# A new order table for attention and the first expert, and fewer preset instructions, in a one-core attention and expert kernel

## The chip, the cores and the metric

The kernel runs on one core of a Trainium2 chip. The metric is the device time of one execution in microseconds, as the median of several runs. Engines are named as in the profile: PE is the matmul engine, DVE the vector engine, ACT the scalar engine, POOL GpSimd, SP the engine that issues the DMAs.

## What is computed

Three stages follow each other: an attention with a coarse and a local part over 2 x 8 heads of 576 positions, a mixture of 8 experts over the 1152 tokens with a gate that is balanced over rows and columns, and one feed-forward layer. Cut to what matters:

```python
# attention, for each of 2 x 8 heads, q, k, v: 576 x 64
q_d, k_d, v_d = (t.reshape(B, H, S // 4, 4, D).mean(axis=3) for t in (q, k, v))
out_up = np.repeat(sm_attn(q_d, k_d, v_d), 4, axis=2)
mask = np.abs(pos[:, None] - pos[None, :]) < 4
out_local = softmax(np.where(mask, scale * q @ k.T, -1e9)) @ v
x = (out_up + out_local).transpose(0, 2, 1, 3).reshape(1152, 512)

# experts: D = 512, F = 1024, E = 8
P = np.exp(x @ w_gate - max)
for _ in range(8):
    P /= P.sum(1, keepdims=True) + 1e-9
    P /= P.sum(0, keepdims=True) + 1e-9
    P *= N / E
out = sum(P[:, e:e + 1] * (np.maximum(x @ w1[e], 0) @ w2[e]) for e in range(E))

# last layer: w_in 512 x 2048, w_out 2048 x 512
h = out @ w_in
return (h * np.tanh(np.log1p(np.exp(h)))) @ w_out
```

## The kernel before

Matrices are multiplied in half precision as a high and a low part each, scaled by powers of two that are found from the data: three products of parts stand for one product. Splitting a matrix takes an ACT instruction for the high part and a DVE instruction for the low part.

The change touches the first stage: attention, and the part of expert 0 that is woven into it. Its work is cut into some 500 **steps**, methods of the class Attention and a few functions beside it. A table, ORDER (line 911), lists them by name, and `run` (line 1346) emits them one after the other. Each engine has a queue of its own and works it off in order, so the table fixes the order on every engine and on the DMA queue of SP; what waits for what is left to semaphores. A name carries its numbers (`TP2.0.1`) and, behind a colon, the engine where there is a choice (`A` for ACT, `V` for DVE, `G` for POOL). The heads go in pairs j = 0 to 7, of which 0 to 3 are batch 0 and 4 to 7 batch 1.

- **LK, LQ, LW, LV**: loads of K and Q of a pair, of the windows of V, of V for the coarse part. **LD0.n, LD1.n, LD2.n**: halves of w1 of expert 0, w2 of expert 0, w1 of expert 1. **LG**: the gate. Tiles come from small pools (four for Q and K, four for V windows, two for raw weights), and a load waits until the tile that it takes over is done with.
- **TPj.n.i**: PE transposes half i of Q (n = 0) or K (n = 1). **TQ, TK** copy it out of PSUM, **SQ, SK** sum four neighbours for the coarse part.
- **QLj.0, .1, .2**: the local scores, 48 small matmuls for each of two heads. **LM, SU, EL, LS, LN, TR, BD**: softmax of these, its transpose and the blocks for the product with V. **QD, DM, ED, DS, DN, AP, AE**: the same for the coarse part.
- **AV, AD**: products with V. **VP, VE, VS, VG, VR, VQ**: coarse V, and what its scale is found from. **UP, XF, XH, XL**: sum of both parts, high and low part of x for this pair.
- **WG, WD, WM, WT, WP, WR, WQ, WE**: the scale of a matrix (squares by PE or ACT, greatest value by DVE, spread over the partitions by PE, powers of two by DVE). **WH, WL**: high and low part of a quarter of expert 0's weights.
- **Mf.c, Rf.c, Hf, If**: one product of the first layer of expert 0 (12 matmuls), its relu, high and low part of the result. They need x of the whole batch. **Nt.f, Et**: the second layer and its way out.
- **FLi**: fill steps. With `A` they do nothing, with `V` they are one matmul on the tile warm, with `G` two (line 1260).

Ahead of the table stand presets: constants on POOL (lines 1271 to 1290, among them an addition on the tile lib, L1290, in front of which POOL stands still) and the identity matrix, the mask and the pooling weights on DVE (emit_consts, from line 536). Behind the table come the rest of expert 0, the other experts and the last layer, which the change leaves alone.

Of the kernel before, what the change touches and what calls it, by code (L numbers as in the profile page):

```python
# [10 lines left out]
F32 = mybir.dt.float32  # L11
# [4 lines left out]
ALU = mybir.AluOpType  # L16
# [5 lines left out]
def attn_moe_moe2_kernel(ctx: ExitStack, tc: tile.TileContext, q, k, v, w_gate, w1, w2, w_in, w_out, out):  # L22
# [495 lines left out]
    pool_w = const.tile([128, 32], F32, name="pool_w")  # L518
    half = const.tile([128, 2], F32, name="half")
# [19 lines left out]
    def emit_consts(t, mask):  # L539
# [3 lines left out]
        nc.vector.memset(ident, 0.0)  # L543
# [6 lines left out]
        for i in range(4):  # L550
            p = slice(32 * i, 32 * i + 32)
            nc.vector.tensor_scalar(out=ident[p, p], in0=d[p, :], scalar1=0.0, scalar2=None, op0=ALU.is_equal)
# [7 lines left out]

# [3 lines left out]
        near = t[:, 5, 0:8]  # L564
        nc.vector.scalar_tensor_tensor(out=near, in0=col[:, 0:8], scalar=-4.0, in1=row[:, 0:8], op0=ALU.mult,
# [3 lines left out]
        for i in range(4):  # L569
            p = slice(32 * i, 32 * i + 32)  # L570
            nc.vector.tensor_scalar(out=pool_w[p, 6 * i:6 * i + 6], in0=near[p, 0:6], scalar1=4.0, scalar2=None,
                                    op0=ALU.is_lt)
# [24 lines left out]
    class Attention:  # L597
# [341 lines left out]


    mm_pools = []
    mm_n = [0]

    def mm_banks(n):
        i = len(mm_pools)
        mm_pools.extend([(ps_pool(f"mm{i}", n), f"mm{i}")] * n)

    def mm_tile():
# [811 lines left out]
```

## Time and profile before

| | us |
|---|---|
| median of 3 runs | 984.0 (983.19 to 984.54) |
| profiled execution | 987.67 |
| its span | 985.9 |
| PE busy in the span | 962.0 |
| DVE busy | 665.2 |
| ACT busy | 517.6 |

The profiled execution is one run beside the timed ones, and its span leaves out what lies ahead of the first instruction and behind the last. PE's busy time is the sum of its matmuls as the trace has them; what is left of the span is waiting. The order table ends at 117 us of the span.

### The profile page before, as it was taken

The numbers are of one execution on the slowest core, as the hardware profiler recorded it, in microseconds if no ns is written. First come the engines' busy times: TensorE is split into PE (matmuls) and PEld (weight loads), VectorE is DVE, ScalarE is ACT, GpSimd is POOL, SyncE is SP. The second block draws the span as 40 slices with busy tenths as digits, with TensorE's granted clock in tenths as the row PEclk, the third lists the DMA queues.
The fourth block names the chain that finished last, engine by engine and source line by source line (L and its number), as shares of the span: only waits on it lengthen the run. The fifth ranks groups of instructions, "written<-read, shape, count | busy, mean of one in ns | idle before, by whom it ended". The sixth has DMA issues, their size and how long they took to land. (4 is left out here: it accounts for less than half of the span.)

```text
span 985.9 us, 19187 instructions
## 1 busy us (share of the span) xinstructions
PE 962.0 (98%) x7925; PEld 653.4 (66%) x7928; DVE 665.2 (67%) x1333; ACT 517.6 (53%) x1000; POOL 60.2 (6%) x114
## 2 busy tenths in 40 slices
PE   6999999999999999999999999999999999999998
PEld 5766674774476467547645754674476667888897
DVE  5877578588677938775994888388756455545531
ACT  4757353766287447728654773567284232433431
POOL 5524200000000000000000000000000000000000
PEclk9999999999999999999999999999999999999999
DMA  8862202022423233240424423232204602000010
GB/s 209 167 146 100 94 6 86 1 87 67 147 88 105 64 137 122 65 155 27 140 65 150 128 66 132 69 120 65 107 4 162 263 1 86 12 12 22 7 60 33
DMA packets 82403, 88.15 MB, mean 89 GB/s; under 512 B 34572, under 2 KB 66700, under 8 KB 81036
## 3 DMA queue, kind: packets, MB, share of 16 engines
q1 hardware_dynamic: 82316, 86.93, 27.6%
q8 instruction: 62, 1.02, 0.4%
q14 instruction: 25, 0.20, 0.1%
HBM read 71.97 MB, written 14.94 MB: 88 GB/s over the span
## 5 line engine op out<-in xcount | busy, mean ns | idle before, releaser
L1124 PE MATMUL mm<-wbh,h 128*128 128x512 f16 x1152 | 353.7, 380 | 2.4 <-ACT h L587 2.4
L1124 PEld LDWEIGHTS <-h 128*128 128x128 f16 x1728 | 168.8, 98 | 196.1 <-ACT h L587 2.9
L1124 PE MATMUL mm<-wbl,h 128*128 128x512 f16 x576 | 219.1, 380 | 0.0
L1093 PE MATMUL mm<-x,wah 128*128 128x288 f16 x672 | 128.1, 286 | 0.0
L1059 DVE SCALAR_TENSOR_TENSOR r<-mm,s 128x288 f32<-128x288 f32 x168 | 75.0, 454 | 71.2 <-PE mm L1093 64.3
L1093 PEld LDWEIGHTS <-wx 128*128 128x128 f16 x1008 | 98.6, 98 | 30.6 <-issue 5.9
L1542 PE MATMUL mm<-xc,win 128*128 128x256 f16 (+1 forms) x960 | 107.6, 262 | 0.0
L1055 ACT ACTIVATE s<-mm 128x288 f32<-128x288 f32 x168 | 66.4, 413 | 75.9 <-PE mm L1093 75.6
L1093 PEld LDWEIGHTS <-wah 128*128 128x128 f16 x896 | 87.7, 98 | 26.5 <-issue 0.6
L1093 PE MATMUL mm<-xt,wx 128*128 128x288 f16 x672 | 97.0, 286 | 4.1 <-DVE r L1059 4.0
L1093 PE MATMUL mm<-x,wal 128*128 128x288 f16 x336 | 96.1, 286 | 0.0
L1542 PEld LDWEIGHTS <-win 128*128 128x128 f16 x960 | 87.2, 98 | 13.3
L1551 ACT ACTIVATE tt<-mm,cf 128x512 f32<-128x512 f32 (+1 forms) x40 | 25.8, 645 | 113.1 <-PE mm L1542 111.3
L1068 DVE SCALAR_TENSOR_TENSOR h<-r,h 128x576 f16<-128x576 f32 x112 | 81.5, 750 | 0.6 <-ACT h L1067 0.6
L1067 ACT ACTIVATE h<-r 128x576 f16<-128x576 f32 x112 | 74.3, 680 | 11.2 <-DVE r L1059 11.0
L1558 DVE TENSOR_TENSOR tt<-tt 128x128 f32<-128x128 f32 x128 | 31.6, 288 | 69.4 <-ACT tt L1551 68.3
L1157 DVE SCALAR_TENSOR_TENSOR acc<-mm,pc,acc 128x512 f32<-128x512 f32 x63 | 47.0, 746 | 33.4 <-PE mm L1124 33.2
L254 ACT ACTIVATE junk<-raw 128x1024 bf16<-128x1024 f32 x52 | 54.9, 1056 | 0.3
L98 POOL PARTITION_ALL_REDUCE ma<-m x25 | 11.4, 458 | 669.5 <-DVE m L258 385.8
L1093 PEld LDWEIGHTS <-wal 128*128 128x128 f16 x448 | 43.8, 98 | 11.1
L1093 PE MATMUL mm<-x,wx 128*128 128x288 f16 x336 | 50.3, 286 | 0.0
L428 ACT ACTIVATE junk<-w 128x512 bf16<-128x512 f32 x32 | 20.1, 629 | 57.2 <-DVE w L421 41.4
(265 smaller groups left out, 1383.8 us busy)
## 6 DMA issues: line engine op xcount, KB each, us to landing
raw<-in_moe_w_dram SPq DMA_DIRECT2D x32, 1024.0 KB, 6.0
f<-in_moe_w_in_dram SPq DMA_DIRECT2D x16, 512.0 KB, 3.7
f<-in_moe_w_out_dram SPq DMA_DIRECT2D x16, 512.0 KB, 3.4
scr<-st SPq DMA_DIRECT2D x32, 256.0 KB, 2.3
scri<-st SPq DMA_DIRECT2D x16, 256.0 KB, 2.5
win<-scri SPq DMA_DIRECT2D x2, 2048.0 KB, 7.6
vw<-in_v_dram SPq DMA_DIRECT2D x30, 96.0 KB, 5.1
qk<-in_k_dram SPq DMA_DIRECT2D x16, 144.0 KB, 3.7
```

Source lines behind the costliest of these rows:

```text
L254: nc.scalar.activation(out=junk, in_=r[:, c * 1024:(c + 1) * 1024], func=AF.Square, accum_out=mx[:, 2 * i + c:2 * i + c + 1])
L428: nc.scalar.activation(out=b, in_=w, func=AF.Square, accum_out=mq[:, f // 8:f // 8 + 1])
L1055: nc.scalar.activation(out=t, in_=ps, func=AF.Copy, scale=HSC)
L1059: nc.vector.scalar_tensor_tensor(out=out, in0=ps, scalar=HSC, in1=r, op0=ALU.mult, op1=ALU.add)
L1067: lows.append((n + 3, lambda: nc.scalar.activation(out=hi, in_=r, func=AF.Relu)))
L1068: lows.append((n + 6, lambda: nc.vector.scalar_tensor_tensor(out=lo, in0=r, scalar=0.0, in1=hi, op0=ALU.max, op1=ALU.subtract)))
L1093: nc.tensor.matmul(ps, lhsT=w.part(wi, a)[:, c:c + 128], rhs=factor(b, bn, xi, i), start=(not before and k == 0), stop=(k == 5), skip_grou ...
L1124: nc.tensor.matmul(ps, lhsT=h[ft][:, hi, t * 128:(t + 1) * 128], rhs=wt[:, ws], start=(ft == 0 and n == 0), stop=(ft == FT - 1 and n == 2))
L1157: nc.vector.scalar_tensor_tensor(out=a, in0=ps, scalar=pc[:, t:t + 1], in1=a, op0=ALU.mult, op1=ALU.add)
L1542: nc.tensor.matmul(ps[:, q_ * n:(q_ + 1) * n], lhsT=win[q_][:, wi, f, ws], rhs=x[:, xi, kk, :], start=(m == 0), stop=(m == 3 * KT - 1))
L1551: nc.scalar.activation(out=tt[:, 0:2 * n], in_=ps, func=AF.Mish, scale=coef[c][:, f:f + 1])
L1558: nc.vector.tensor_tensor(out=a[o], in0=a[u], in1=a[v], op=op)
```

## The change

ORDER gets a new text with the same 511 steps: all 30 fill steps are in it, but four of them now issue five matmuls together, where six issued seven. Steps move in the table, and some change their engine: five more TQ, four TK and two SQ are on DVE, one SK, one AE and one H fewer. The presets are rewritten: the identity matrix and the pooling weights are made in one instruction each from a pattern of 32 columns and a tile block that says which rows belong to which 32; the tile warm is set on DVE instead of POOL, half comes from block, and the POOL instructions stand in another order with lib ahead of most. The table, cut to its first line on both sides:

```diff
+    block = const.tile([128, 4], F32, name="block")
...
-        nc.vector.memset(ident, 0.0)
...
-        for i in range(4):
-            p = slice(32 * i, 32 * i + 32)
-            nc.vector.tensor_scalar(out=ident[p, p], in0=d[p, :], scalar1=0.0, scalar2=None, op0=ALU.is_equal)
+        near = t[:, 5, 0:32]
+        nc.vector.tensor_scalar(out=near, in0=d, scalar1=0.0, scalar2=None, op0=ALU.is_equal)
+        nc.vector.tensor_tensor(out=ident.rearrange("p (b c) -> p b c", b=4), in0=near.unsqueeze(1).to_broadcast([128, 4, 32]),
+                                in1=block.unsqueeze(2).to_broadcast([128, 4, 32]), op=ALU.mult)
...
+        nc.vector.memset(warm, 1.0)
...
-        for i in range(4):
-            p = slice(32 * i, 32 * i + 32)
-            nc.vector.tensor_scalar(out=pool_w[p, 6 * i:6 * i + 6], in0=near[p, 0:6], scalar1=4.0, scalar2=None,
-                                    op0=ALU.is_lt)
+        nc.vector.tensor_scalar(out=near, in0=near, scalar1=4.0, scalar2=None, op0=ALU.is_lt)
+        nc.vector.tensor_tensor(out=pool_w[:, 0:24].rearrange("p (b c) -> p b c", b=4),
+                                in0=near.unsqueeze(1).to_broadcast([128, 4, 6]),
+                                in1=block.unsqueeze(2).to_broadcast([128, 4, 6]), op=ALU.mult)
...
-        "LK0 TP0.1.0 LQ0 FL5:V LK1 TP0.1.1 TP0.0.1 LK2 TP0.0.0 TK0.1:A TK0.0:A FL23:G LQ1 LD0.1 TQ0.1:A LQ2 TQ0.0:V "
...
+        "LK0 TP0.1.1 TP0.1.0 LQ0 LQ1 TK0.1:A TP0.0.0 TQ0.0:V TP0.0.1 TK0.0:A LK1 TQ0.1:V LD0.1 QL0.0 QL0.1 QL0.2 "
...
-        nc.gpsimd.memset(warm, 1.0)
-        nc.gpsimd.memset(half, 0.0)
+        lib = pools["keep"].tile([128, 16], F32, name="lib")
+        nc.gpsimd.memset(block, 0.0)
         for i in range(4):
-            nc.gpsimd.memset(half[32 * i:32 * i + 32, i % 2:i % 2 + 1], 1.0)
-        nc.gpsimd.memset(ones, 1.0)
-        nc.gpsimd.memset(ss, 0.0)
-        nc.gpsimd.memset(pool_w, 0.0)
+            nc.gpsimd.memset(block[32 * i:32 * i + 32, i:i + 1], 1.0)
+        nc.gpsimd.memset(lib, 0.0)
+        nc.gpsimd.memset(pool_w[:, 24:32], 0.0)
...
+        nc.gpsimd.tensor_tensor(out=lib[:, 0:8], in0=lib[:, 0:8], in1=lib[:, 8:16], op=ALU.add)
+        nc.gpsimd.tensor_tensor(out=half, in0=block[:, 0:2], in1=block[:, 2:4], op=ALU.add)
+        for i in range(2):
+            nc.gpsimd.memset(keep["ad"][i].rearrange("p h a g c -> p (h a g) c")[:, :, 24:32], 0.0)
+        nc.gpsimd.memset(ones, 1.0)
+        nc.gpsimd.memset(ss, 0.0)
         emit_fields()
-        lib = pools["keep"].tile([128, 16], F32, name="lib")
-        nc.gpsimd.memset(lib, 0.0)
-        nc.gpsimd.tensor_tensor(out=lib[:, 0:8], in0=lib[:, 0:8], in1=lib[:, 8:16], op=ALU.add)
```

What this does to the engines' queues is shown at three places. First the DMA queue of SP from its start, before (qk are the tiles of Q and K, raw those of weights, vw the V windows):

```order
L607 DMA qk<-in_k_dram 96x6x64 x2
L607 DMA qk<-in_q_dram 96x6x64 x2
L607 DMA qk<-in_k_dram 96x6x64 x4
L607 DMA qk<-in_q_dram 96x6x64 x2
L158 DMA raw<-in_moe_w_dram 128x2x1024
L607 DMA qk<-in_q_dram 96x6x64 x2
L626 DMA vw<-in_v_dram 29x64
L626 DMA vw<-in_v_dram 32x11x64
L626 DMA vw<-in_v_dram 32x12x64 x3
L158 DMA raw<-in_moe_w_dram 128x2x1024
L607 DMA qk<-in_k_dram 96x6x64 x2
```

And the same queue in the new order:

```order
L608 DMA qk<-in_k_dram 96x6x64 x2
L608 DMA qk<-in_q_dram 96x6x64 x4
L608 DMA qk<-in_k_dram 96x6x64 x2
L158 DMA raw<-in_moe_w_dram 128x2x1024 x2
L608 DMA qk<-in_k_dram 96x6x64 x2
L608 DMA qk<-in_q_dram 96x6x64 x2
L608 DMA qk<-in_k_dram 96x6x64 x2
L627 DMA vw<-in_v_dram 29x64
L627 DMA vw<-in_v_dram 32x11x64
L627 DMA vw<-in_v_dram 32x12x64 x11
L608 DMA qk<-in_q_dram 96x6x64 x4
```

Both halves of w1 now stand ahead of K2 and Q2, and three V windows ahead of Q4 and Q3. Second, PE from its start, before (at and aty are the PSUM tiles of transposes, fill that of the fill steps, att that of the scores):

```order
L704 MATMUL at<-ident,qk 128x96 x3
L1263 LDWEIGHTS warm
L1263 MATMUL fill<-warm 128x512
L704 MATMUL aty<-ident,qk 128x96 x6
L704 MATMUL at<-ident,qk 128x96 x3
L1263 LDWEIGHTS warm
L1263 MATMUL fill<-warm 128x512
```

And the same in the new order:

```order
L705 MATMUL aty<-ident,qk 128x96 x3
L705 MATMUL at<-ident,qk 128x96 x6
L705 MATMUL aty<-ident,qk 128x96 x3
L737 LDWEIGHTS ident_82
L737 MATMUL att<-mask,ident_82 128x192
```

The fill matmuls between the first transposes and the scores are gone. Third, DVE in front of the last low part of x of batch 0 (x<-xf, four instructions, the last is XL3; wal are low parts of w1, sl softmax steps), before:

```order
L243 SCALAR_TENSOR_TENSOR wal<-raw,sc_w_0_705,wah 128x1024
L764 TENSOR_TENSOR sl<-att,lmx 128x384
L889 TENSOR_TENSOR xf<-att,up 128x2x6x48
L899 SCALAR_TENSOR_TENSOR x<-xf,sx_1051,x 128x576 x3
L889 TENSOR_TENSOR xf<-att,up 128x2x6x48
L243 SCALAR_TENSOR_TENSOR wal<-raw,sc_w_0_705,wah 128x1024
L899 SCALAR_TENSOR_TENSOR x<-xf,sx_1051,x 128x576
```

And in the new order:

```order
L765 TENSOR_TENSOR sl<-att,lmx 128x384
L900 SCALAR_TENSOR_TENSOR x<-xf,sx_1074,x 128x576
L1171 TENSOR_REDUCE m_1180<-wg_r 128x1
L900 SCALAR_TENSOR_TENSOR x<-xf,sx_1074,x 128x576
L890 TENSOR_TENSOR xf<-att,up 128x2x6x48
L110 TENSOR_REDUCE mrow<-at 1x1
L890 TENSOR_TENSOR xf<-att,up 128x2x6x48
L900 SCALAR_TENSOR_TENSOR x<-xf,sx_1074,x 128x576 x2
```

Two low parts of w1 that stood here have moved further ahead, and a step for the gate's scale (mrow) stands between.

## Rows read from the trace of the kernel before

**Rows 1.** The page: the span's busy times and instructions of each engine.

```profile
PE 962.0 (98%) x7925; PEld 653.4 (66%) x7928; DVE 665.2 (67%) x1333; ACT 517.6 (53%) x1000; POOL 60.2 (6%) x114
```

**Rows 2.** Stages: stretch in us, length, busy us (instructions), PE clock, DMA share, GB/s.

```profile
0.00:20.00 20.00, 13.42 (x285) 10.40 (x286) 12.20 (x45) 8.37 (x24) 8.88 (x44) 0.91 0.86 216
20.00:40.00 20.00, 16.78 (x426) 13.63 (x424) 14.39 (x36) 13.31 (x43) 11.76 (x14) 0.91 0.80 164
40.00:52.00 12.00, 10.97 (x345) 8.52 (x344) 11.72 (x22) 9.45 (x23) 5.22 (x7) 1.00 0.98 221
52.00:62.00 10.00, 7.70 (x81) 5.58 (x81) 5.82 (x12) 5.58 (x19) 2.98 (x5) 0.83 1.17 227
62.00:117.00 55.00, 55.00 (x746) 35.66 (x742) 41.97 (x83) 31.53 (x80) 19.19 (x19) 1.00 0.17 57
```

**Rows 3.** PE's timeline: start, duration, line, tiles, count, wait in front with releaser.

```profile
23.40 0.69 PE L743 MATMUL att<-kt,qt 64*32 64x32 f32 x43 [2.18 <-issue]
...
33.27 0.25 PE L743 MATMUL att<-kt,qt 64*32 64x32 f32 x4 [0.51 <-issue]
...
52.55 0.41 PE L969 MATMUL mm<-x,wah 128*128 128x288 f16 x2
...
57.10 0.28 PE L969 MATMUL mm<-x,wal 128*128 128x288 f16 x1 [2.30 <-issue]
...
117.02 2.35 PE L1192 MATMUL lp<-wg_hl,x 128*128 128x16 f16 x80
```

**Rows 4.** Three more stretches, in the columns of rows 2.

```profile
23.39:57.09 33.70, 29.34 (x756) 23.40 (x759) 29.73 (x63) 23.60 (x66) 16.34 (x20) 0.95 0.90 195
...
50.00:57.09 7.09, 4.79 (x131) 3.65 (x128) 6.91 (x12) 4.59 (x16) 2.68 (x5) 1.00 1.19 281
...
57.50:60.90 3.40, 3.40 (x18) 2.40 (x16) 0.76 (x1) 2.22 (x5) 0.00 (x0) 0.52 1.20 200
```

**Rows 5.** The page: instruction queue (packets, MB), and loads by tile (issues, KB each).

```profile
q8 instruction: 62, 1.02, 0.4%
...
raw<-in_moe_w_dram SPq DMA_DIRECT2D x32, 1024.0 KB, 6.0
...
vw<-in_v_dram SPq DMA_DIRECT2D x30, 96.0 KB, 5.1
qk<-in_k_dram SPq DMA_DIRECT2D x16, 144.0 KB, 3.7
```

**Rows 6.** Start: the first K load's issue, the time that such loads take, PE, POOL.

```profile
0.72 0.94 SPq L607 DMA_DIRECT2D qk<-in_k_dram  x2
...
DMA to landing us min/median/max: 2.6/2.6/2.6
...
4.15 0.71 PE L704 MATMUL at<-ident,qk 96*128 96x96 f32 x3 [4.15 <-DVE mask_t L556]
...
10.80 0.20 POOL L1290 TENSOR_TENSOR lib<-lib 128x8 f32<-128x8 f32 x1 [7.47 <-DVE lmx L759]
```

**Rows 7.** PE's timeline at full clock: two TP, mask, QL part, AP.

```profile
39.13 0.83 PE L704 MATMUL at<-ident,qk 96*128 96x96 f32 x6
39.80 0.33 PE L736 MATMUL att<-mask,ident 128*128 128x192 bf16 x2
40.06 0.35 PE L743 MATMUL att<-kt,qt 64*32 64x32 f32 x32
40.34 0.46 PE L844 MATMUL at<-ident,ad 72*96 72x72 f32 x4
```

**Rows 8.** DVE from 30.4 to 52.5 us by line: count, busy us, mean ns.

```profile
L243 DVE SCALAR_TENSOR_TENSOR wal<-raw,sc_w,wah 128x1024 f16<-128x1024 f32 x4 | 5.4, 1344 | 0.0
L899 DVE SCALAR_TENSOR_TENSOR x<-xf,sx,x 128x576 f16<-128x576 f32 x4 | 3.1, 805 | 0.0
L889 DVE TENSOR_TENSOR xf<-att,up 128x576 f32<-128x576 f32 x4 | 3.0, 745 | 0.2 <-ACT up L587 0.2
```

**Rows 9.** PE's waits from 110 to 165 us: line, releaser, total us, count, longest.

```profile
PE mm L1124 <- ACT h L587: 2.4, 1, 2.4
```

More of the change, by code (lines that the diff above doesn't have):

```diff
@@ L559, in emit_consts @@
         nc.scalar.activation(out=mask, in_=edge.unsqueeze(1).to_broadcast([128, G, 32]), func=AF.Copy)
+        nc.vector.memset(warm, 1.0)
         nc.vector.memset(mask[0:32, 0, 0:3], SHUT)
         nc.vector.memset(mask[96:128, G - 1, 27:32], SHUT)
-        near = t[:, 5, 0:8]
-        nc.vector.scalar_tensor_tensor(out=near, in0=col[:, 0:8], scalar=-4.0, in1=row[:, 0:8], op0=ALU.mult,
+        near = t[:, 5, 0:6]
+        nc.vector.scalar_tensor_tensor(out=near, in0=col[:, 0:6], scalar=-4.0, in1=row[:, 0:6], op0=ALU.mult,
                                        op1=ALU.add)
@@ L1282, in attn_moe_moe2_kernel @@
             nc.gpsimd.memset(keep["qt"][i][:, S:S + 8], 0.0)
-            nc.gpsimd.memset(keep["ad"][i].rearrange("p h a g c -> p (h a g) c")[:, :, 24:32], 0.0)
         A = [Attention(b, pools, at_tile, at2_tile) for b in range(B)]
```

52 rows, old and new, of the table ORDER are left out of this document.

## The prediction

> **What bounds the kernel now.** I read the page first, then the stages, then what stops PE. TensorE is busy 962.0 of 985.9 us at almost full clock [rows 1], so some 24 us of idle time are there to win, and the change reaches only those ahead of the gate's matmuls at 117.0 us, where the order table ends [rows 3]. The stages [rows 2] tell where they lie. From 62 to 117 us PE is busy 55.00 of 55.00: no order wins there. From 0 to 40 us PE has 30.2 us of work and the DMA engines are 0.86 and 0.80 busy: this part goes at the pace of the loads. From 40 to 52 us DVE is busy 11.72 of 12: VectorE sets the pace, since the first product of expert 0 needs all of x of batch 0, whose last low part (XL3) is DVE work. From 52 to 62 us PE is busy 7.70 of 10 at a clock of 0.83, with DVE at 5.82: something else stops PE. [Rows 3] show it: 2.18 us of standstill in front of 23.40, 2.30 us in front of 57.10, each in the middle of a run of equal matmuls and waiting for no engine ("issue"). Between the two stand 1515 loads and matmuls [rows 4], six times 252; queue q8 brings 62 instruction packets of 16 KB [rows 5] for PE's 15,853 loads and matmuls [rows 1], 256 to a packet. Both stops are ends of an instruction block whose successor had not come.
>
> On this the Trainium skill (Runtime: NRT & Kernel Launch, section Instruction fetch mechanics) also has blocks of 16 KiB or 256 instructions, but calls their crossing mostly hidden. The trace agrees on the block, not on the hiding: [rows 3] have 2.30 us in the open. By that rule nothing of the kind would stand in the new order and term 3 below would be -4.0, which is a rival's value; by the rows it hangs on what the loads do just then.
>
> **The presets.** ident took five DVE instructions and takes two now. But the first transposes, at 4.15 us, also need the first K load, whose second half is issued at about 1.2 us and takes 2.6 us or a little more [rows 6]: it is there close to 4 us. I take 0, between 0 and -0.3. POOL comes free for attention only at 10.80, behind 7.5 us of standstill in front of lib [rows 6]; lib stands some 1 us earlier in the new order, but about 1 us of memsets (ad, ones, ss, the fields) has moved behind it: 0. The two fill matmuls fewer ran where PE was waiting anyway.
>
> **The loads up to 36 us.** The new table takes both halves of expert 0's w1 ahead of K2 and Q2. Sizes are in [rows 5]: a Q or K load is two of 144 KB, a V window four of 96 KB, a half of w1 1024 KB. Ahead of TP2.0.1 now stand six Q/K loads and two halves, 3.87 MB. At the 216 GB/s of the first 20 us, or the 190 of the first 40 [rows 2], that is 17.9 to 20.4 us: PE will stand idle in front of TP2.0.1, where it was working before. It then has 8.6 us of work up to TP3.0.1, which needs Q3: 5.93 MB, 29.8 to 31.2 us. From there 4.1 us to TP4.1.1, which needs K4: 6.91 MB, 35.8 to 36.4 us. (PE work is counted by steps, start to start in [rows 7]: 0.33 for a TP, 0.28 for a QL part, 0.26 for its mask; by the same timeline about 0.3 for AP, 0.64 for AD and QD, 0.85 AV, 0.6 VP, 0.4 VG, 1.0 WG.) At 36.1 us the kernel before has 20.8 us of table work done, the new one 19.1 to 19.5: it is behind here, not ahead.
>
> The wait in front of TP2.0.1 also drops the clock, as the 2.30 us did before: [rows 4] have 0.52 between 57.5 and 60.9. The same again is 1.7 us, and lies under the wait for Q3, so I take 0. The Trainium skill (TensorE: Matmul & The Clock Gate, Part 1) says that the array is throttled until activity releases it, which speaks against dropping fill matmuls; the clock rows agree with it, and by the rule alone the sum would be 1.7 us worse.
>
> **VectorE up to the first product.** From TQ3.1, behind Q3, the new table has these DVE steps up to and with XL3: three low parts of w1 at 1.34 us, four XL at 0.80, four XF at 0.75 [rows 8], four TQ, a pooled sum, two transposes, the softmax steps and the scale of x: 21.7 us by the trace's durations. The same count for the kernel before, from 30.4 us (LS2) to XL3's end at 52.45, gives 22.2, and it took 22.1. So the first product comes 21.6 us behind about 30.9, at 52.5 us, as before (52.55, [rows 3]). **Term 1: 0**, from -1.5 (Q3 at 29.8, DVE without a gap) to +1.5 (Q3 at 31.2, and waits of DVE on PE). By its own work PE is there at 51.3 and does not decide.
>
> **Behind the first product.** The PE work left is 0.3 us more: two transposes (TP6.0.0, TP6.0.1) have moved behind it, the pair WQ3 ahead of it. **Term 2: +0.3.**
>
> The stop at 57.10 cost 2.30 us and then the clock, 0.83 over ten us or 1.7 us [rows 2]: 4.0 together. Counting loads and matmuls, the same block begins in the third product (M0.1) now, in the second (also M0.1) before. The one ahead of it begins near 50 us in both: [rows 4] have 259 loads and matmuls from 50.00 to 57.09, in the new order TP6.1.1 stands there. So it took 7.1 us from the crossing to the next block, of which PE's work filled some 4.5. Now the need comes at 52.5 + 2.9 = 55.4 instead of 54.8. The loads just then are the same: half of w2 (LD1.0), LW5, LQ7. LW5 waits for AV3, near 47.7; LD1.0 can go a little ahead of it, so its data is perhaps half a us earlier. The block then comes at 56.5 to 57.0, and 1.1 to 1.6 us of the stop stay, and the clock with it. **Term 3: -1.2**, between -4.0 (the block is in time) and +0.3 (later by that). The stop at 23.40 goes, since the block behind QL1.2 arrives while PE waits for Q2; it lay under the loads and is worth 0.
>
> VectorE has more to do: five TQ, four TK, two SQ have moved to it, less has left, some 5 us net, most in expert 0's first stage. Up to TK7.0, which QL7.0 needs, DVE has 22.4 us by prices, PE 24.4. From 62 to 117 us it was busy 41.97 of 55 [rows 2]; now it needs nine tenths of the time up to there. **Term 4: +0.3** for PE waiting on it, from 0 to 2.5.
>
> From 117 us on the code is the same, and what stops PE there, 2.4 us for ACT h [rows 9], comes from an order that starts from the same place: 0.
>
> **Sum**: 0 + 0.3 - 1.2 + 0.3 = -0.6 us. The profiled execution took 987.67 us around a span of 985.9; the median of the three timed ones is 984.0. The terms are differences of parts, so they go on the median: 983.4.
>
> **Rivals.** *The block is in time.* If LD1.0 is through by 50 us, or PE crosses into the block ahead when it is, the next block comes while PE works through this one, as at the crossings between the two stops, the worst of which cost 0.51 us at 33.27 [rows 3], and term 3 is -4.0: 0.3 - 4.0 + 0.3 = -3.4, and with term 1 between -1.5 and +0.5 from -4.9 to -2.9, so 979.1 to 981.1. For it: in the new order DMA has a gap near 42 us (LW4 waits for AV0), so less stands in the queues. Against it: LQ6, LW6 and LV4 are ahead of LD1.0. *VectorE is late.* Slower than before: the copies moved from ACT to DVE stand in line behind low parts of 1.3 us; Q3 comes at 31.2 or later, XL3 ends at 54 (+1.5), and in the first stage PE waits for TK7.0 and for banks (+2); with the stop as it was, 1.5 + 0.3 - 0.5 + 2 = +3.3, between +2 and +4.5: 986 to 988.5. It decides once DVE's gaps between 18 and 52 us have grown by more than 1.5 us.
>
> **How the numbers follow.** The forecast, part of the stop remaining, covers -2.6 to +1.5 us and gets 0.50; the block in time 0.32; VectorE late 0.18. A measurement of this kernel tells some 0.2%, 2 us, from no change: faster is below 982.0, slower above 986.0. The forecast has 0.08 below 982.0 and 0.42 within; the block in time lies below; of VectorE late 0.01 is within. Faster 0.40, same 0.43, slower 0.17. The range goes from 978.6, half a us beyond the first rival's end for the presets and faster loads, to 986.6 in the slower case; some 0.2 stays outside. The forecast's own range is 981.4 to 985.5.
>
> **What would show it.** In the profile after: an idle PE in front of TP2.0.1, near 18 us, as its longest wait in the first 40 us; the first product (mm from x and wah) between 51 and 54 us; an "issue" wait of 1 to 2 us in the third product, then a clock of one half; DVE over 0.85 busy from there to 80 us; the gate's matmuls at 116 to 117 us. I am wrong on the loads if TP2.0.1 starts before 17 us or Q3 is there before 29; on VectorE if the first product comes by 50 or after 55; on the block if there is no "issue" wait over 0.5 us behind the first product, and then the time is the first rival's. If all these agree and the time does not, the difference lies behind 117 us, where I have put 0.

## The result: 0.5% slower, and the profile after

The changed kernel took 989.28 us (median of five, 988.51 to 991.05) against 984.0 before (five, 982.85 to 985.6): a ratio of 1.0055, 95% interval 1.0039 to 1.007. A second comparison, later and with twelve runs of it and 35 of the kernel before, gave 988.59 against 985.16 us, 1.0021 with 0.9998 to 1.0043. The range of the prediction ended at 986.6, and no change or a small gain had been the likely case. By the medians the change is a loss of 3 to 5 us. The ratios take in all runs and not the medians alone, and the second interval just reaches no change, so the sign of the loss is surer than its size.

The busy times of the page say nothing of it; in the columns of [rows 1]:

```profile
PE 963.2 (98%) x7923; PEld 654.7 (66%) x7926; DVE 665.8 (67%) x1340; ACT 513.6 (52%) x990; POOL 53.8 (5%) x112
```

The stages do; in the columns of [rows 2], and one more stretch, 15 to 25 us:

```profile
0.00:20.00 20.00, 11.91 (x247) 9.20 (x247) 10.39 (x36) 5.25 (x15) 6.43 (x41) 1.00 0.94 223
20.00:40.00 20.00, 17.01 (x329) 13.26 (x332) 13.58 (x38) 12.35 (x34) 8.25 (x12) 0.91 0.75 147
40.00:52.00 12.00, 10.81 (x319) 8.21 (x321) 10.51 (x25) 7.15 (x23) 9.42 (x11) 1.00 0.56 120
52.00:62.00 10.00, 9.46 (x230) 7.12 (x223) 9.37 (x20) 4.38 (x12) 3.48 (x5) 1.00 0.93 213
62.00:117.00 55.00, 55.00 (x753) 36.61 (x752) 41.93 (x84) 34.53 (x92) 14.11 (x18) 1.00 0.31 85
...
15.00:25.00 10.00, 7.51 (x110) 5.85 (x107) 2.83 (x10) 1.48 (x7) 2.64 (x6) 1.00 0.76 155
```

From 15 to 25 us VectorE is busy for 2.83 of 10 us, and TensorE needs 7.51 us for only 110 matmuls. From 40 to 52 us, where the loads had been at 0.98 and VectorE at 11.72 of 12 [rows 2], both have gaps now. TensorE's timeline (start, duration, line, tiles, the wait in front) shows where time is lost and where not:

```profile
18.88 0.71 PE L705 MATMUL aty<-ident,qk 96*128 96x96 f32 x3 [1.43 <-DMA qk<-in_q_dram]
20.15 0.74 PE L705 MATMUL aty<-ident,qk 96*128 96x96 f32 x3 [0.55 <-DVE qt L592]
...
26.04 0.41 PE L705 MATMUL aty<-ident,qk 96*128 96x96 f32 x3 [0.16 <-issue]
...
31.25 0.70 PE L845 MATMUL at<-ident,ad 72*96 72x72 f32 x8 [1.15 <-ACT kt L588]
...
34.25 0.68 PE L705 MATMUL aty<-ident,qk 96*128 96x96 f32 x3
...
58.06 0.42 PE L970 MATMUL mm<-x,wah 128*128 128x288 f16 x2
...
61.19 0.28 PE L970 MATMUL mm<-x,wah 128*128 128x288 f16 x1 [0.26 <-issue]
...
119.29 2.35 PE L1193 MATMUL lp<-wg_hl,x 128*128 128x16 f16 x80
```

TP2.0.1 waits for Q2 until 18.88, as forecast. TP3.0.1 starts at 34.25, where 29.8 to 31.2 was forecast; no load stands in front of it. The first product of expert 0 is at 58.06 instead of 52.55 [rows 3], 5.5 us late. The stop of 2.30 us is gone: 0.26 us is the longest "issue" wait behind the first product. The gate's matmuls are 61.23 us behind the first product.

The transposes are a clock of their own. The granted clock of the profile has one stretch at 0.50, the half level, from 31.96 to 35.37 us, and a group of three that starts in it, TP3.0.1, takes 0.68 us; behind it, at 1.00, such groups take 0.47. Until 25 us all of them take 0.68 to 0.74 us, and from 26.04 on 0.41. There the granted clock reads 1.00 all the same (the stages above, 0 to 25 us), so the record doesn't seem to hold the level at which an execution starts. That the first 25 us are at half clock is read here from the durations, and "half clock" and "full clock" ahead of 30 us mean that below, unless a granted clock is given.

VectorE waits for TensorE four times between 15 and 26 us, 7.2 us in all:

```profile
17.53 0.56 DVE L760 TENSOR_REDUCE lmx<-att 128x12 f32<-128x384 f32 x1 [2.01 <-PE att L744]
19.63 0.46 DVE L592 TENSOR_SCALAR qt<-aty 128x288 f32<-128x288 f32 x1 [1.54 <-PE aty L705]
22.63 0.29 DVE L203 TENSOR_REDUCE mx<-at 128x1 f32<-128x128 f32 x1 [1.62 <-PE at L584]
25.16 0.28 DVE L110 TENSOR_REDUCE mrow<-at 1x1 f32<-1x128 f32 x1 [2.05 <-PE at L106]
...
35.36 0.44 DVE L592 TENSOR_SCALAR qt<-aty 128x288 f32<-128x288 f32 x1
...
37.18 0.46 DVE L592 TENSOR_SCALAR qt<-at 128x288 f32<-128x288 f32 x1 [0.56 <-PE at L705]
...
55.55 1.74 DVE L900 SCALAR_TENSOR_TENSOR x<-xf,sx,x 128x576 f16<-128x576 f32 x2
```

The row at 35.36 is TQ3.1, the one at 37.18 is TQ4.0 ("the copy of Q4" below); the last row holds XL3, which ends at 57.29. From TQ3.1 to there it took 21.9 us, where 21.6 was forecast. The stretch has the forecast length; it starts 4.5 us late.

### The profile page after: what moved, and what is told of

The parts are those of the page before. It is cut to its first block, busy times and chain, and to the rows that moved or that the text cites. A ratio compares the mean times of both kernels' runs of the same rounds, so it can differ in the third digit from the quotient of the medians.

```text
span 987.5 us, 19175 instructions
## 1 busy us (share of the span) xinstructions
PE 963.2 (98%) x7923; PEld 654.7 (66%) x7926; DVE 665.8 (67%) x1340; ACT 513.6 (52%) x990; POOL 53.8 (5%) x112
## 5 line engine op out<-in xcount | busy, mean ns | idle before, releaser
L1094 PEld LDWEIGHTS <-wx 128*128 128x128 f16 x1008 | 98.6, 98 | 30.5 <-issue 5.9
```

The lines of the kernel that those rows point to most:

```text
L1094: nc.tensor.matmul(ps, lhsT=w.part(wi, a)[:, c:c + 128], rhs=factor(b, bn, xi, i), start=(not before and k == 0), stop=(k == 5), skip_grou ...
```

## The experiments

One theory stood against several rivals. The theory: the new order reaches the copy of Q4 late, because TensorE idles and runs at half clock up to 25 us. The rivals: the presets, ScalarE's order, VectorE's own work. Besides, the profile of before lay 3.7 us above its median, which had to be understood. Times in one table first (us); "full clock" is the start of the first x3 group of transposes that takes 0.52 us or less, after which the fast ones go on; the medians of before are those timed together with the kernel.

| kernel | full clock from | copy of Q4 | first product | from there to the gate | span | median (before) |
|---|---|---|---|---|---|---|
| before, its first profile | (drops between) | | 52.55 | 64.47 | 985.9 | 984.0 |
| e_before_again | 20.5 | | 52.46 | 60.46 | 981.5 | 985.0 (984.97) |
| e_presets_only | 12.34 (a drop near 26) | | 52.14 | 61.39 | 982.8 | 984.64 (984.97) |
| e_old_nofill | 20.65 | | 51.99 | 61.77 | 982.6 | 985.55 (986.72) |
| after | 26.04 (a drop at 32) | 37.18 | 58.06 | 61.23 | 987.5 | 989.28 (984.0) |
| e_after_again | 28.81 | 35.87 | 56.13 | 61.04 | 986.4 | 988.59 (985.16) |
| e_order_only | 29.25 | 36.14 | 56.41 | 61.22 | 986.8 | 986.81 (984.97) |
| e_tk3 | 30.85 | 38.58 | 58.96 | 61.53 | 989.2 | 989.52 (985.16) |
| e_w1_back | 18.10 | 33.16 | 53.70 | 60.80 | 983.2 | 987.27 (984.97) |
| e_w1_act | 17.89 | 33.43 | 53.69 | 60.80 | 984.4 | 987.07 (985.16) |
| e_fills | 18.30 | 32.99 | 53.75 | 60.80 | 984.4 | 987.57 (985.16) |
| e_fills_act | 10.12 | 32.78 | 54.13 | 61.31 | 983.7 | 988.07 (985.28) |

Single executions of one kernel differ by several us, by whether a stop for instructions or a stretch of half clock falls into them; so the stages of the profiles carry the argument here, and the medians only bound it.

**e_before_again**, the kernel before once more, no edit.

> The kernel before once more, unchanged. Its profiled execution took 987.67 us, 3.7 us above the median 984.0 of its timed runs, and held at 57.10 us a wait for instructions of 2.30 us, with the clock at half from 57.6 to 61.0 us. Theory 'the stop is not in the timed runs': a second profile has a span of about 982.2 (984.0 less the 1.8 that lie around the span), no wait named issue over 0.5 us between 53 and 62 us, and the gate's matmuls at about 113 us instead of 117.0. Rival 'the stop is there each time, and the profiled run lost its 3.7 us elsewhere or profiling itself adds them': the second profile has the same wait of 2 us or more behind the first product and the gate's matmuls at 117.

Its first product and the gate's matmuls in TensorE's timeline, then two stretches in the columns of [rows 2], the first of them the stage that had held the stop:

```profile
52.46 0.41 PE L969 MATMUL mm<-x,wah 128*128 128x288 f16 x2
...
112.92 2.35 PE L1192 MATMUL lp<-wg_hl,x 128*128 128x16 f16 x80
```

```profile
52.00:62.00 10.00, 10.00 (x175) 7.77 (x174) 9.44 (x22) 6.06 (x21) 5.56 (x8) 1.00 0.95 207
...
15.00:25.00 10.00, 9.51 (x273) 7.80 (x274) 6.60 (x19) 6.41 (x25) 6.97 (x10) 1.00 0.93 204
```

PE is busy 10.00 of 10 from 52 to 62 us, at full clock: no stop. From the first product to the gate it took 60.46 us, against 64.47 in the first profile [rows 3]. The difference of 4.01 us is the stop and the clock behind it, and makes up most of the 4.4 us between the spans (985.9 and 981.5). This execution took 983.3 us, and the 35 runs of before timed beside it have a median of 984.97, with 26 under 986; three are above the first profile's 987.67 (in two sets timed later 12 of 35 and 10 of 29). So the whole stop is not in the usual execution. A smaller one can be: the median lies 1.7 us above this execution, and the timed runs left no trace that would tell. The last row is for comparison with after: 273 matmuls from 15 to 25 us where the new order has 110, and VectorE at 6.60 us instead of 2.83.

**e_after_again**, the changed kernel once more, no edit.

> The changed kernel once more, unchanged. Theory 'the first product's time decides, and each kernel then takes 60.5 to 61.4 us from it to the gate's matmuls unless a wait for instructions stops it': first product at 56.4 (as in the new order with the old presets) to 58.1 us, gate 61.2 us behind it, span 985.5 to 987.5, median of the timed runs 987 to 989, 2 to 4 us above the kernel before. Rival 'the 5.3 us of the first comparison are mostly the spread of runs': under 1 us above the kernel before.

All as the theory had it, but for a first product 0.3 us ahead of its range: 56.13, the gate 61.04 us behind it, span 986.4, and 3.4 us between the medians. Of the 1.9 us by which the first product is ahead of the first profile's, 1.0 comes from Q2, which let TP2.0.1 start at 17.84 instead of 18.88. Another 0.3 us lies between there and the copy of Q4, where the first profile's clock fell at 32 us, and 0.6 between the end of XL3 and the product, whose cause is open. The rows stand beside those of e_fills below.

**e_presets_only and e_order_only**, the two halves of the change apart: the first has the new presets with the old string ORDER, the second the old presets with the new one.

> The new presets with the old step order. Theory 'the order costs it all': 984 us, as before (within 1), first product of expert 0 at 52 to 53 us. Rival 'the presets cost it' (the fill matmuls wait for warm, which VectorE now clears later, and the clock rises later): 986 to 989 us, first matmuls later than 4.15 us or TensorE at half clock beyond 9 us.

> The old presets with the new step order. Theory 'the order costs it all': 988 to 990 us, first product at 57 to 59 us, TensorE at half clock until about 25 us. Rival 'the presets cost it': 984 to 986 us. A sum of two parts would show as 986 to 988 here and 985 to 987 for the presets alone.

The first product in each, and the transposes of the second:

```profile
52.14 0.41 PE L970 MATMUL mm<-x,wah 128*128 128x288 f16 x2
```

```profile
18.10 0.71 PE L704 MATMUL aty<-ident,qk 96*128 96x96 f32 x3 [0.95 <-DMA qk<-in_q_dram]
19.36 0.74 PE L704 MATMUL aty<-ident,qk 96*128 96x96 f32 x3 [0.55 <-DVE qt L591]
...
25.63 0.69 PE L704 MATMUL aty<-ident,qk 96*128 96x96 f32 x3 [0.33 <-issue]
...
29.25 0.41 PE L704 MATMUL at<-ident,qk 96*128 96x96 f32 x3
...
56.41 0.42 PE L969 MATMUL mm<-x,wah 128*128 128x288 f16 x2
```

The presets alone change nothing (1.0007, 0.9984 to 1.0031). The order alone has the late first product and the half clock up to 25.63 and beyond. Its median, 986.81, is below the 988 to 990 that was expected, and its ratio, 1.001 (0.9988 to 1.0032), doesn't tell it from before; it is the profile that puts the loss on the order. By the times alone a sum of two parts (986 to 988 here, 985 to 987 for the presets) is met in the first half and missed in the second.

**e_w1_back**, part of the load order undone.

```diff
-... TP1.1.0 LD0.0 LK2 ... FL10:A LQ2 TQ1.1:V ... WD0.1 WG0.0 DS0 ... FL21:A WD0.0 TP2.0.0 WT0
+... TP1.1.0 LK2 ... FL10:A LQ2 LD0.0 TQ1.1:V ... WD0.1 DS0 ... FL21:A TP2.0.0 WG0.0 WD0.0 WT0
```

> The changed kernel with the second half of w1 of expert 0 (LD0.0) requested behind Q2 instead of ahead of K2, and its squares and maxima (WG0.0, WD0.0) behind the transposes of step 2. Theory 'the two halves of w1 ahead of K2 and Q2 make TensorE idle and slow until 25 us': the wait in front of TP2.0.1 at 18.9 us is gone (it starts at 14.5 to 16), the first product comes 2 to 4 us sooner (54 to 56 us), 985 to 987 us in all. Rival 'the wait only moves' (WG0.0 then waits for the later half, and the chain of w1's scale, WP0 to WH0, comes later with it): first product at 57 to 60 us and 988 to 991 us.

```profile
16.81 0.74 PE L705 MATMUL aty<-ident,qk 96*128 96x96 f32 x3
18.10 0.47 PE L705 MATMUL aty<-ident,qk 96*128 96x96 f32 x3 [0.55 <-DVE qt L592]
...
53.70 0.42 PE L970 MATMUL mm<-x,wah 128*128 128x288 f16 x2
```

TP2.0.1 starts at 16.81 without a wait, later than the 14.5 to 16 expected, because TensorE's own work only then lets it. The first product is 2.4 us ahead of e_after_again and 4.4 ahead of after, 0.3 us ahead of the 54 to 56 expected. But two things changed at once: the wait is gone, and the clock is at full from 18.10. The timed median (987.27, ratio 1.0035, 1.0009 to 1.0061) shows little of it and is above the 985 to 987 expected.

**e_fills**, the clock without the loads: seven fill matmuls more in the changed kernel, and the loads where the change puts them.

```diff
-... TP0.1.0 LQ0 ... TP0.0.1 TK0.0:A ... QL1.0 FL10:A LQ2 ... QL1.2 TP2.0.1
+... TP0.1.0 FL30:V LQ0 ... TP0.0.1 FL31:G TK0.0:A ... QL1.0 FL10:G LQ2 ... QL1.2 FL32:G TP2.0.1
```

> The changed kernel with seven more fill matmuls on TensorE where it waits anyway: one behind TP0.1.0, two behind TP0.0.1, two behind QL1.0 (FL10 with G for A) and two in front of TP2.0.1. Theory 'the half clock until 25 us costs it' : the x3 transposes take 0.47 us in place of 0.74 from about 12 us on, and the first product comes 1.5 to 3 us sooner than in the changed kernel (55 to 56.5 us). Theory 'VectorE's idle time ahead of the loads of step 2 costs it': Q2 still lands at 18.7 us, full clock gives at most 1 us, first product 57 to 58, and time within 1 us of the changed kernel's.

This kernel: TensorE's timeline, then VectorE's at TQ3.1, the copy of Q4 and XL3:

```profile
17.86 0.60 PE L1264 MATMUL fill<-warm 128*128 128x512 bf16 x2
18.30 0.41 PE L705 MATMUL aty<-ident,qk 96*128 96x96 f32 x3
19.26 0.47 PE L705 MATMUL aty<-ident,qk 96*128 96x96 f32 x3 [0.55 <-DVE qt L592]
...
30.42 0.41 PE L705 MATMUL aty<-ident,qk 96*128 96x96 f32 x3
...
53.75 0.42 PE L970 MATMUL mm<-x,wah 128*128 128x288 f16 x2
```

```profile
31.49 0.44 DVE L592 TENSOR_SCALAR qt<-aty 128x288 f32<-128x288 f32 x1
...
32.99 0.46 DVE L592 TENSOR_SCALAR qt<-at 128x288 f32<-128x288 f32 x1 [0.58 <-PE at L705]
...
51.43 1.74 DVE L900 SCALAR_TENSOR_TENSOR x<-xf,sx,x 128x576 f16<-128x576 f32 x2
```

The same of e_after_again, VectorE's at the copy of Q4 alone:

```profile
17.84 0.71 PE L705 MATMUL aty<-ident,qk 96*128 96x96 f32 x3 [0.97 <-DMA qk<-in_q_dram]
19.11 0.74 PE L705 MATMUL aty<-ident,qk 96*128 96x96 f32 x3 [0.55 <-DVE qt L592]
...
25.37 0.69 PE L705 MATMUL aty<-ident,qk 96*128 96x96 f32 x3
...
56.13 0.42 PE L970 MATMUL mm<-x,wah 128*128 128x288 f16 x2
```

```profile
35.87 0.46 DVE L592 TENSOR_SCALAR qt<-at 128x288 f32<-128x288 f32 x1 [0.58 <-PE at L705]
```

TP2.0.1 starts 0.46 us later than in e_after_again, and the copy of Q4 comes 2.9 us earlier: 14.7 us behind TP2.0.1 instead of 18.0. What differs there is the clock: from 18.30 on the transposes take 0.41 to 0.47 us. The first product gains 2.4 us on e_after_again and 4.3 on after; at 53.75 it is ahead of the 55 to 56.5 that the theory had asked for, and this with both halves of w1 still ahead of K2 and Q2. (The full clock came at 18 us and not at 12, as it had it.) So the half clock, not the arrival of Q2, costs about 3 us between TP2.0.1 and the copy of Q4. That the place of the loads matters because it leaves TensorE with little to do until then is argued and was not tested by itself.

The medians show only 1.0 us of the 2.4 (987.57 and 988.59). A likely reason is that later falls of the clock differ from run to run. Among the runs with a mean granted clock of 0.997 or more, which is a mean that doesn't hold the first stretch, the median is 986.55 with the fills (seven of 12 runs), 988.9 without (five of 12) and 984.57 for before (15 of 35): 2.35 of 4.3 us come back, much as in the profiles. These runs were picked out afterwards, and they are few.

**e_tk3**, ScalarE's order.

```diff
-... WE0 VG1 WH0.1 BD0:V ... VG0 WH0.0 SU2 TK3.0:A FL23:A
+... WE0 VG1 BD0:V ... VG0 SU2 TK3.0:A WH0.1 WH0.0 FL23:A
```

> The changed kernel with WH0.1 and WH0.0 (rounding of w1 on ScalarE) behind TK3.0 instead of ahead of it, so that the copy of K3 doesn't wait behind them. Theory 'ScalarE's order costs part of it': the wait of 1.15 us of TensorE at 31.25 us on kt is gone and the first product comes about 1 us sooner. Rival 'VectorE is behind by then anyway': the wait is gone, the first product is where it was (within 0.4 us).

```profile
19.70 0.71 PE L705 MATMUL aty<-ident,qk 96*128 96x96 f32 x3 [4.71 <-DMA qk<-in_q_dram]
...
34.54 0.64 PE L676 MATMUL at<-vw,pool_w 128*32 128x128 f32 x12 [1.74 <-ACT atd L588]
...
58.96 0.42 PE L970 MATMUL mm<-x,wah 128*128 128x288 f16 x2
```

The wait of 1.15 us for the copy of K3 is gone, and a wait of 1.74 for another of ScalarE's copies (atd) has come in its place. In this execution Q2 was there only at 19.7 us, and the clock, at full at 10.55 us, fell within the wait of 4.71 and came back at 30.5. Behind the copy of Q4 all was as ever (20.4 us). No gain shows: from TP2.0.1 to the copy of Q4 it took 18.9 us, against 18.0 in e_after_again. But the clock was at half for most of that, so a part of a us for ScalarE's order is not ruled out; it doesn't explain the loss.

**e_w1_act**, VectorE's work: e_w1_back, and besides

```diff
-... TK1.1:V SQ0:V TK1.0:V ... TQ2.1:V ... BD0:V
+... TK1.1:A SQ0:G TK1.0:A ... TQ2.1:A ... BD0:G
```

> As the run with the second half of w1 behind Q2 (first product at 53.70 us), and five steps besides go from VectorE back to where the old order has them: TK1.1, TK1.0 and TQ2.1 to ScalarE, SQ0 and BD0 to GpSimd, some 2 us of VectorE's work. Theory 'the first product comes when VectorE has done its 40 us of work and its idle time ahead of it' (38.7 + 13.8 = 52.5 in the kernel before, 40.1 + 18.0 = 58.1 in the changed one, 40.25 + 13.45 = 53.7 with w1 back): 51.5 to 52.5 us and 983 to 984.5 in all, as the kernel before or up to 1.5 us faster. Rival 'TensorE or ScalarE set it once the loads are back in place': 53 to 54 us, 985 or more.

The theory of VectorE's sum fell. VectorE's busy time ahead of the first product went from 40.25 to 37.15 us, and the first product stayed at 53.69; what VectorE no longer had to do it waited, 16.5 us in all instead of 13.4. The five steps lie ahead of the copy of Q4, and that copy waits for TensorE (33.43 here, 33.16 there).

**e_old_nofill**, the reverse test: the kernel before without its early fills (FL5 and FL12 from V, one matmul, to A, none; FL23 from G, two, to A).

> The kernel before without its four early fill matmuls on TensorE (FL5, FL23, FL12 set to none). Theory 'a half clock before 25 us costs the first product 2 to 4 us in either order': the x3 transposes take 0.7 us until 20 us or later and the first product comes at 54 to 56 us. Rival 'the old order has slack there' (in its second profile the clock was at half until 17.9 us, with the first product at 52.46 all the same): first product at 52 to 53 us, and 984 to 986 us in all.

```profile
16.55 0.74 PE L704 MATMUL aty<-ident,qk 96*128 96x96 f32 x3
...
20.65 0.47 PE L704 MATMUL at<-ident,qk 96*128 96x96 f32 x3
...
51.99 0.41 PE L969 MATMUL mm<-x,wah 128*128 128x288 f16 x2
...
55.99 0.41 PE L969 MATMUL mm<-x,wah 128*128 128x288 f16 x2 [1.26 <-issue]
```

The old order doesn't need its fills: 985.55 against 986.72 us (0.9985, 0.996 to 1.001). Its TensorE has 9.52 us of work between 15 and 25 us, in its own order, and the full clock is there by 20.65 all the same. That a half clock before 18 us costs 2 to 4 us in either order is refuted: in the old order the first product is at 51.99 and 52.46 with full clock from 20.5 us, and at 52.14 with full clock from 12.34; in the new order e_fills_act, at full clock from 10.12, has the copy of Q4 at 32.78, and e_fills, from 18.30, at 32.99. What counts is the stretch behind it.

**e_w1_fills and e_combo**: both repairs at once, and in e_combo two steps behind the copy of Q4 taken from VectorE besides, without the two fills in front of TP2.0.1 (FL32 at A).

```diff
-... TQ4.0:V SQ3:V ... TQ5.1:A TQ5.0:V
+... TQ4.0:V SQ3:G ... TQ5.1:A TQ5.0:A
```

> Both repairs of the changed kernel at once: the second half of w1 behind Q2, and seven fill matmuls. Each alone gave a first product at 53.7 us, with the copies of Q4 on VectorE at 33.0 to 33.2 us. Theory 'both did the same thing, they brought the full clock at 18 us instead of 25 to 28': together again 53 to 54 us. Rival 'one repaired the loads and the other the clock, two causes': together 51 to 52.5 us, and 983 to 984.5 in all.

> As the run with both repairs, and behind the copy of Q4 VectorE loses two steps: the copy TQ5.0 goes to ScalarE and the pooling SQ3 to GpSimd (0.46 and 0.74 us). In all profiles of the new order the first product came 20.3 to 20.9 us behind that copy. Theory 'from there on VectorE's work sets it': 19.1 to 19.7 us behind it, first product at 52 to 53 us or 1.2 us ahead of the run with both repairs. Rival 'TensorE and ScalarE set it': unchanged, 20.3 or more.

Neither could be decided in the profiles. Both profiled executions are among the longest of their kernels (994.2 and 997.6 us, with medians of 989.05 and 986.38): the clock was at full from 9.4 us on, fell to half after 29 us, and stayed there. The stretches of that, of e_combo and then of e_w1_fills, in the columns of [rows 2]:

```profile
29.20:40.00 10.80, 9.46 (x152) 6.88 (x150) 7.18 (x13) 5.35 (x19) 6.21 (x7) 0.50 0.89 141
40.00:63.40 23.40, 23.16 (x396) 17.03 (x395) 12.56 (x29) 9.85 (x28) 7.38 (x10) 0.50 0.59 150
```

```profile
29.90:47.00 17.10, 15.98 (x280) 11.96 (x281) 10.37 (x24) 7.85 (x29) 9.13 (x12) 0.50 0.71 129
```

A group of three transposes in the first of them, on TensorE's timeline of e_combo:

```profile
32.28 0.74 PE L705 MATMUL at<-ident,qk 96*128 96x96 f32 x3
```

Here the granted clock is 0.50 and the group takes what such groups take ahead of 25 us in the changed kernel. The first product came at 65.09 and 61.67 us (the second with a wait for instructions of 2.22 us in front of 58.66 besides). It shows what the half clock costs when it lasts. The medians say that both repairs together are no better than one: 2.3 us above before for e_w1_fills; e_combo's lies 0.3 below, but its ratio is 1.0017 (0.9985 to 1.0049).

**e_fills_act**: e_fills with the two steps of the last diff.

> The changed kernel with the seven fill matmuls of the earlier run, and behind the copy of Q4 VectorE loses the copy TQ5.0 (to ScalarE) and the pooling SQ3 (to GpSimd), 0.46 and 0.74 us. Theory 'full clock from 18 us brings the copy of Q4 at 33 us, and from there VectorE's work alone sets the first product': copy of Q4 at 32.8 to 33.4 us (35.9 to 37.2 in the changed kernel), first product 19.1 to 19.7 us behind it (20.3 to 20.9 in the other runs of the new order), that is at 52 to 53 us; gate's matmuls 60.8 to 61.4 us after that; 984.5 to 986 us in all. Rival 'TensorE and ScalarE set the last stretch': 20.3 us or more behind the copy, 53.5 us or later.

The copy of Q4 came at 32.78, the second profile with fills that has it at 33 us. XL3 ended 20.0 us behind it, where e_fills had 20.2: 1.2 us of VectorE's work less gave 0.2. The rival holds: in the last stretch too VectorE also waits for others. The first product at 54.13 had a wait for instructions in front of it besides:

```profile
51.33 0.38 PE L1264 MATMUL fill<-warm 128*128 128x512 bf16 x1 [1.22 <-issue]
```

No version of the new order came out ahead of the kernel before, clear of noise.

## Why the prediction was wrong

**The presets, 0: right.** 984.64 us with them alone, against 984.97.

**The loads: right where they arrive, wrong in what follows.** TP2.0.1 started at 18.88 and 17.84 us in the two profiles, where 17.9 to 20.4 was forecast (17.84 is at its edge), and no longer wait stands in front of TensorE behind its first load, as said. The step that failed is the next: 8.6 us of work up to TP3.0.1, counted with the prices of [rows 7], which stand at full clock, and one fall of the clock for 1.7 us, taken as 0 because it would lie under the wait for Q3. TensorE wasn't falling from full clock there; in both profiles it had not reached it yet. (In e_tk3 it did fall in that wait, and stayed at a granted 0.50 from 16.8 to 30.5 us.) From TP2.0.1 to TP3.0.1 it took 15.4 us (18.88 to 34.25), so Q3 was no cover: no wait for a load stands in front of TP3.0.1. Even at full clock it took 12.1 us (e_fills, 18.30 to 30.42), since the waits on the other engines in between, the longest 1.14 us on ScalarE's copy of K3, had no price either; that ends within the 29.8 to 31.2 forecast for Q3, and so costs little.

**Term 1, 0 (-1.5 to +1.5): measured +3.7 between the second profiles, +5.5 between the first.** The length of VectorE's stretch was met: 21.6 us from TQ3.1 to XL3's end, measured 21.9, and 21.7 with full clock (e_fills, 31.49 to 53.17). That is in part luck. It was counted as VectorE's work, but VectorE is busy only 19.49 of those 21.7 us, where in the kernel before it was 20.70 of 22.05; less work and more waiting made up for each other, and in e_fills_act 1.2 us of work less gave 0.2. Of the loss some 2.4 us are the clock, by e_fills against e_after_again. The 1.25 us from the forecast 52.5 to the 53.75 of e_fills are a TQ3.1 at 31.49 instead of 30.9 and 0.6 us between XL3's end and the product, which the sum had at nothing. What sets these two was not settled, and so it stays open whether more than the clock would have to change for the new order to reach the old.

**Terms 2 and 4, +0.6 together: the sum was right, the reason for term 4 was not.** From the first product to the gate it took 61.23 and 61.04 us, before 60.46 without the stop: +0.6 to +0.8. But TensorE doesn't wait for VectorE there: it is busy 60.97 and 60.96 us of these, against 60.46. It is 0.5 us more work, where 0.3 was forecast, and in the first profile the 0.26 us of "issue" besides. VectorE's busy time up to the gate grew by 2.7 us (84.07 in e_before_again, 86.78 in e_after_again), not by some 5, although two UP and one E went to it too, which the lists of the change leave out.

**Term 3, -1.2: the price was right, the base was wrong.** The stop and its clock were put at 4.0 us, and the two profiles of before differ by 4.01 in that stage. In the new order the block was in time (0.26 us), as the first rival said and against the forecast of 1.1 to 1.6. But the sum was set on the median of 984.0, and e_before_again shows that an execution near it need not hold the stop. The sentence "the terms are differences of parts, so they go on the median" holds only for parts that the median's executions have too. The 3.7 us by which the profiled execution exceeded the median were on the table, and were about the size of the stop; that was the hint. Against e_before_again the term is 0. The median of 984.0 is 0.7 us above that execution, and the 984.97 timed beside it 1.7, so little of the 4.0 was there to gain.

**Behind 117 us, 0: right.** From the gate to the end of the span it took 868.2 and 869.2 us after, 868.9 and 868.6 before.

Measured, between the second profiles: +3.67 to the first product, +0.58 to the gate, +0.65 behind it, 4.9 in all, the spans 986.4 and 981.5.

**The rivals.** "VectorE is late" had the place (a first product past 54) and the sign, its time (986 to 988.5) ended 0.1 and 0.8 us short of the two medians, and its condition was met: VectorE's gaps between 18 and 52 us grew from 6.0 to 9.5 us. Its mechanism was not: the five steps that e_w1_act took back from VectorE had cost nothing, and VectorE waited for TensorE. A rival on the clock was missing, although the text weighed it: the Trainium skill (TensorE: Matmul & The Clock Gate, Part 1) says that the array is throttled until activity releases it, which the trace bears out with transposes of 0.68 to 0.74 us up to 25 us; that rule was given 1.7 us and no chance. On the other page of the Trainium skill that was weighed (Runtime: NRT & Kernel Launch, section Instruction fetch mechanics), the crossing at the first products was mostly hidden in the new order, as it says (0.26 us, and none over 0.2 in the second profile); with the old order it stood open with 2.30 us, with 1.26, or not at all, from one execution to the next.

## What to carry to other kernels

Before a stop in a profile is entered as a gain, see whether the executions that make the median have it: a profiled run that lies above the median by about the size of the stop is a strong hint that they don't, and a second profile shows it. And price TensorE's steps at the clock that they will run at: here, in the order that brought both halves of w1 ahead of K2 and Q2, the transposes turned fast at 26 to 29 us instead of 20.5, and each of them up to there cost up to 1.6 times as much (0.74 us for 0.47). Read that from durations, since the granted clock of the profile said 1.00. A few fill matmuls ahead of the step showed this, as a test; as a repair they made the loss smaller in the profile, by 1.0 us in the median, and didn't remove it.

## What the runs showed of the hardware

The half level of the clock can last with TensorE at work. In e_combo it held from 29.2 to 63.4 us, over 23.4 us of which PE was busy for 23.16; the matmuls agree with it, 0.74 us for three transposes. In the first profile of before none of its falls lasted over 3.5 us. The Trainium skill (TensorE: Matmul & The Clock Gate, Part 1) warns that the records of the clock have been seen to be unreliable, and the gate stuck at a quarter for 50 us and more. Here the level is one half, for 34 us, and the matmuls' durations bear that record out. They don't bear out the 1.00 that it reads for the first 25 us of the changed kernel.

The same instruction block of the same kernel came in time in one execution of before and 2.30 us late in another. An earlier block was 2.18 us late in front of 23.40 us in the first profile of before and 0.27 in front of 23.57 in the second; with the old order and the new presets it was 2.81 us late in front of 23.29. Such a stop is no property of an order alone.
